# An attention layer feeding a mixture of experts: other pieces at both ends, half a superblock transposed, and a new order

## The chip, the cores and the metric

The kernel runs on one core of a Trainium2 chip. The metric is the time on the device in microseconds (us), lower is better. Engines are named as the profile names them: PE (TensorE: matmuls and transposes), DVE (VectorE), ACT (ScalarE), POOL (GpSimd) and SP (SyncE, which here only issues transfers). Each runs its own instructions strictly in the order in which they stand. All large transfers are issued by SP on one queue and are spread over the 16 DMA engines of the core.

## The reference

The output of an attention block with 32 learned queries is the input of a mixture of experts that sends each token to one expert.

```python
def mab(q, kv):                        # B 4, N 11456, m 32, C 128
    s = scale * (q @ kv.transpose(0, 2, 1))
    a = np.exp(s - s.max(-1, keepdims=True))
    a /= a.sum(-1, keepdims=True) + 1e-09
    return a @ kv
h = mab(I, x)                          # 32 queries over all tokens of a batch
x = mab(x, h).reshape(B * N, C)        # every token over the 32 rows of h
...
logits = (x / |x|) @ en.T / tau        # 8 experts
gate = softmax(logits) at its argmax
out[mask] = gate_w[mask, None] * (np.maximum(x[mask] @ w1[e], 0.0) @ w2[e])
```

## The kernel before, in words

Each of the 4 batches is cut into 6 superblocks of 1920 tokens (the last of a batch has 1856), so there are 24, numbered g = 0 to 23; batch b owns g = 6b to 6b+5. A superblock is 15 blocks of 128 tokens.

**Stage 1** (`stage1(g)`) needs every token of a batch. `load g` brings the superblock with channels on the partitions. The same tokens with tokens on the partitions come in one of two ways: for the g in `LOADED`, `loadx g` brings them from a second layout in memory; for the others PE transposes block by block (`xt g.h`) and ACT or DVE copies the result out of PSUM (`xe g.h`). `s1 g` are the scores against the 32 queries, `e1 g` the exponentials (ACT), `e1t g` a transpose (DVE), and `h g` adds to the batch's sum in PSUM.

**Between the stages** (`finish(b)`) a batch's h is normalised, small tables are made of it (`hd`, `tab`), the batch's expert is picked (`pick b`, DVE), and `loadw b` brings that expert's two weight matrices, 512 KB each. SP reads the expert's number from memory before it can issue them. `G b` and `K b` on PE multiply the weights with the small tables.

**Stage 2** (`stage2(g0, size)`) runs over groups of one or two superblocks: `s2 g` scores (PE), `am`, `e2` exponentials (ACT), `ud` two products (PE), `w`, `n2`, `dt`, and a chain of small steps up to the gate `gf`; then `F` (DVE), `eg` (POOL or DVE), `out g` (PE), two evictions `oe g.h` from PSUM (ACT or DVE) and `store g` (SP).

What sets the order is written out by hand. `ORDER` is a list of all steps; each engine runs its own steps in that order, and SP its loads and stores. `AT` gives each buffer its slot (18 slots of 960 KB hold superblocks, in and out). `BY_DVE` names the steps that DVE runs in place of their usual engine. `FILL` puts matmuls of zeros, whose result nobody reads, in front of some steps. `SPLIT` names the superblocks whose last steps and stores go in two pieces (blocks 0 to 7, 8 to 14). A load also waits until the load six before it has landed (`DEPTH`). A chain of checks at the end (`ck2` to `verdict`) sets a counter that each engine reads before the program ends.

Of the kernel before, what the change touches and what calls it, by code (L numbers as in the profile page):

```python
# [45 lines left out]
load 7, e1t 5, en7, rz 0.0, rz 0, hde 0, xe 5.0, h 5, hsb 0, s1 6, hd 0, m1 6, s1 7, sha 1, load 9, shb 1, hdc 0,
tab 0, s2 0, tabc 0, am 0, sta 0, stb 0, load 8, loadx 7, loadx 6, s2 4, vote 0, s2 1, e1 7, pick 0, e1 6, pz 1,
e2 0, e2 4, s2 2, tabs 0.0, e1t 7, loadw 0, load 10, tw 0, s2 3, s2 5, e2 2, tabs 0.1, tabs 0, am 4, am 5, e2 3,
e2 1, load 11, load 12, ud 0, am 3, uc 0, pad 17, oh 0, am 2, am 1, e1t 6, ld 0, pad 11, w 0, loadx 8, e2 5, ud 1,
ud 2, ud 3, ud 4, ud 5, uc 2, n2 0, w 1, dt 0, n2 1, zk 0, uc 3, s1 8, load 13, load 14, ln 0, ex 0, e1 8, w 2,  # L50
# [5 lines left out]
sha 2, fac 4, out 0, oe 0.0, e1t 11, zc 1, e1t 10, den 4, shb 2, oe 0.1, S 2, zr 1, rz 1.0, rz 1, h 10, h 11, lg 4,
el 4, hsb 1, v 2, gf 2, out 1, e1 12, hd 1, hdc 1, s1 14, e1t 12, F 3, S 4, pz 2, oe 1.0, s2 6, v 4, F 2, tab 1,
gf 4, tabc 1, s1 13, am 6, vote 1, pick 1, tabs 1.0, eg 3, s2 8, am 8, eg 2, sta 1, tabs 1.1, stb 1, ld 1, py 2,
e1 14, s2 9, s2 7, oe 1.1, tabs 1, am 9, e1 13, F 4, am 7, e2 6, e2 8, out 3, tw 1, oe 3.0, F 5, ad 1, e2 9, eg 4,
oe 3.1, ud 8, store 1, w 8, ud 9, e2 7, oh 1, loadw 1, dt 8, xt 12.1, xe 12.1, w 9, xt 17.0, xt 12.0, xe 17.0,  # L60
n2 8, out 4, xe 12.0, oe 4.0, eg 5, n2 9, s2 11, s2 10, load 18, md 1, oe 4.1, mdc 1, e2 11, e2 10, am 10, out 2,
ln 8, zk 1, ex 8, oe 2.0, ud 6, ud 7, uc 7, oe 2.1, ck1 0, am 11, e1t 13, dt 6, s1 16, G 1, w 6, GT 1, h 12, h 13,
e1 16, gs 1, n2 6, loadx 14, loadx 16, w 7, z 8, fac 8, load 21, gk 1, den 8, ud 10, ud 11, e1t 16, n2 7, ln 6,
ex 6, load 19, store 2, z 6, lg 8, out 5, fac 6, store 4, w 10, w 11, marg 1.0, den 6, h2 1, e1t 14, oe 5.0, lg 6,
oe 5.1, el 6, s1 18, K 1, Kc 1, s1 15, h 14, s1 17, n2 11, dt 10, K4 1, el 8, e1 15, S 6, xt 17.1, n2 10, m1 18,
marg 1.1, v 6, marg 1, e1t 15, S 8, mq 1, gf 6, xe 17.1, F 6, mx 1, xt 18.0, F 7, e1 17, K4c 1, h 15, zc 2,
load 20, h 16, xe 18.0, e1t 17, zr 2, sha 3, rz 2.0, z 10, eg 6, v 8, loadx 22, gf 8, shb 3, rz 2, out 6, h 17,
e1 18, s1 19, F 8, e1t 18, hsb 2, hd 2, hdc 2, ck1 1, oe 6.0, pz 3, oe 6.1, eg 7, xt 18.1, e1 19, ln 10, ex 10,
fac 10, den 10, out 7, xe 18.1, tab 2, tabc 2, F 9, oe 7.0, oe 7.1, store 0, eg 8, lg 10, el 10, s2 12, am 12,
vote 2, pick 2, s2 14, s2 13, s1 20, eg 9, sta 2, tabs 2.0, tabs 2.1, s2 15, stb 2, S 10, load 23, loadx 19, e2 12,  # L70
am 14, tabs 2, tw 2, e2 13, e1 20, e2 14, e1t 19, v 10, e2 15, oh 2, out 8, oe 8.1, am 13, loadw 2, gf 10, F 11,
F 10, am 15, store 5, ud 14, ud 15, uc 14, oe 8.0, eg 10, dt 14, ud 12, ud 13, w 12, n2 12, out 9, w 13, load 22,
s2 17, oe 9.0, h 18, s1 21, e2 17, dt 12, s2 16, G 2, uc 15, oe 9.1, am 17, n2 13, h 19, ld 2, eg 11, loadx 20,
w 14, e1t 20, ad 2, am 16, md 2, GT 2, n2 14, gs 2, mdc 2, e1 21, e2 16, ln 12, out 10, ex 12, oe 10.1, w 15, z 12,
store 7, store 9, store 3, ud 16, ud 17, marg 2.0, n2 15, fac 12, pad 23, gk 2, marg 2.1, e1t 21, marg 2, den 12,
zk 2, mq 2, store 6, lg 12, w 17, dt 16, w 16, K 2, s1 22, store 8, ln 14, oe 10.0, store 10, Kc 2, K4 2, e1 22,
el 12, h2 2, z 14, S 12, xt 21.0, K4c 2, xe 21.0, ex 14, n2 16, n2 17, xt 21.1, xe 21.1, xt 23.1, xt 23.0, py 3,
s1 23, v 12, fac 14, den 14, lg 14, xe 23.1, gf 12, F 13, F 12, ln 16, ex 16, hde 3, z 16, el 14, fac 16, den 16,
lg 16, xe 23.0, e1 23, el 16, eg 12, h 20, h 21, S 14, out 11, oe 11.1, e1t 22, v 14, e1t 23, mx 2, zc 3, h 22,
zr 3, h 23, S 16, v 16, rz 3.0, hsb 3, rz 3, gf 14, gf 16, F 14, out 12, oe 12.0, eg 13, hd 3, oe 11.0, hdc 3,  # L80
tab 3, tabc 3, s2 18, F 15, vote 3, pick 3, tabs 3.0, tabs 3.1, oe 12.1, store 11, eg 15, tw 3, out 13, am 18,
sta 3, tabs 3, oe 13.1, oe 13.0, eg 14, F 16, s2 19, s2 21, stb 3, loadw 3, e2 21, am 19, am 21, F 17.1, e2 18,
e2 19, s2 20, out 14, am 20, eg 16, ud 18, ud 19, w 18, F 17.0, oe 14.1, e2 20, oe 14.0, out 15, w 19, store 13,
oe 15.1, ud 20, ud 21, uc 20, dt 18, n2 19, n2 18, ln 18, dt 20, w 21, store 14, oe 15.0, eg 17.0, out 16, ex 18,
oe 16.1, s2 22, G 3, oe 16.0, out 17.0, s2 23, eg 17.1, z 18, w 20, n2 20, fac 18, den 18, lg 18, el 18, n2 21,
ln 20, GT 3, gs 3, S 18, gk 3, am 22, store 12, v 18, oe 17.0.1, ex 20, oe 17.0.0, am 23, gf 18, K 3, Kc 3,
out 17.1, z 20, e2 22, fac 20, den 20, F 18.0, K4 3, lg 20, F 18.1, oe 17.1.1, el 20, eg 18.1, oe 17.1.0, K4c 3,
F 19, ud 22, e2 23, S 20, v 20, gf 20, out 18.1, oe 18.1.1, oe 18.1.0, w 22, dt 22, ud 23, uc 23, eg 18.0,
store 15, out 18.0, F 21, dt 23, eg 19, oe 18.0.0, store 16, store 17.1, z 22, oe 18.0.1, store 17.0, ld 3, n2 22,
ad 3, F 20.1, F 20.0, eg 21, w 23, ln 22, out 19, oe 19.1, oe 19.0, ex 22, fac 22, store 18.1, eg 20.0, ck1 2,  # L90
# [805 lines left out]
```

## Time and profile before

| what | value |
|---|---|
| time, median of 3 runs | 165.62 us (163.82 to 166.64) |
| time of the profiled execution | 165.58 us |
| its span, first to last instruction | 163.4 us |
| PE busy | 152.0 us (93%) |
| DVE, ACT, POOL busy | 128.0, 111.4, 68.2 us |
| bytes moved | 62.33 MB, mean 382 GB/s |
| matmuls, of them transposes of blocks | 2086, 195 |

The profiled execution took 2.2 us more than its span, and it lies 0.04 us from the median of the three runs, so sums made against it hold for the median too. Busy shares are averages over the whole span; the rows below are cut by stage, because the load on each engine changes along the way. A busy PE is not a PE at its peak: the ends of its matmuls are modelled.

### The profile page before, as it was taken

The numbers are of one execution on the slowest core, as the hardware profiler recorded it, in microseconds if no ns is written. First come the engines' busy times: TensorE is split into PE (matmuls) and PEld (weight loads), VectorE is DVE, ScalarE is ACT, GpSimd is POOL, SyncE is SP. The second block draws the span as 40 slices with busy tenths as digits, with TensorE's granted clock in tenths as the row PEclk, the third lists the DMA queues.
The fourth block names the chain that finished last, engine by engine and source line by source line (L and its number), as shares of the span: only waits on it lengthen the run. The fifth ranks groups of instructions, "written<-read, shape, count | busy, mean of one in ns | idle before, by whom it ended". The sixth has DMA issues, their size and how long they took to land.

```text
span 163.4 us, 5394 instructions
## 1 busy us (share of the span) xinstructions
PE 152.0 (93%) x2086; PEld 82.2 (50%) x2090; DVE 128.0 (78%) x326; ACT 111.4 (68%) x244; POOL 68.2 (42%) x181
## 2 busy tenths in 40 slices
PE   7999999999999999999999999999999998898900
PEld 5658695334976634536585433738643232233400
DVE  0437664789997999989986899999878989897820
ACT  3063661966884697783878993789896899997520
POOL 8700000236664265216242634843636074884200
PEclk9999999999999999999999999999999999999995
DMA  5999999999999999999999999999997999999970
GB/s 154 394 412 423 421 423 417 418 367 419 420 423 423 412 423 382 416 421 372 305 424 331 364 413 424 422 427 431 412 394 261 330 425 419 412 373 416 408 307 19
DMA packets 10732, 62.33 MB, mean 382 GB/s; under 512 B 1352, under 2 KB 1360, under 8 KB 10704
## 3 DMA queue, kind: packets, MB, share of 16 engines
q1 hardware_dynamic: 10512, 61.94, 94.8%
q8 instruction: 17, 0.28, 0.7%
q14 instruction: 11, 0.09, 0.1%
q10 hardware_dynamic: 192, 0.02, 0.1%
HBM read 38.49 MB, written 23.46 MB: 379 GB/s over the span
## 4 chain that ended last, share of the span: by engine, by line
PE 80%; ACT 10%; DVE 3%; issue 2%; POOL 1%; DVEq 0%; POOLq 0%
PE psum L293 62%; PE psum L396 14%; ACT big L290 6%; PE psum L717 4%; ACT E L562 1%; ACT s L592 1%; ACT gf L609 1%; DVE F L620 1%; POOL E2g L622 0%; DVE am L557 0%; ACT s L593 0%; DVE Wp L582 0%; ACT ex L602 0%; DVE DT L587 0%; DVE E2g L622 0%
## 5 line engine op out<-in xcount | busy, mean ns | idle before, releaser
L290 ACT COPY big<-psum 128x960 f32<-128x960 f32 (+4 forms) x67 | 55.7, 853 | 20.9 <-PE psum L396 12.0
L622 POOL TENSOR_TENSOR E2g<-E,F 128x480 f32<-128x480 f32 (+2 forms) x24 | 25.9, 1084 | 21.8 <-PE psum L293 12.8
L293 PE MATMUL psum<-E2g,K 32*128 32x480 f32 (+2 forms) x232 | 27.5, 543 | 1.2 <-ACT big L290 0.3
L293 PE MATMUL psum<-big,ind 128*32 128x480 f32 x192 | 24.5, 571 | 0.1
L293 PE MATMUL psum<-big,E1T 128*32 128x128 f32 x720 | 24.5, 273 | 0.0
L396 PE MATMUL psum<-ident,big 128*128 128x128 f32 x195 | 24.1, 280 | 0.0
L396 PEld LDWEIGHTS psum<-ident,big 128*128 128x128 f32 x195 | 21.8, 144 | 4.1 <-issue 3.0
L293 PEld LDWEIGHTS psum<-big,E1T 128*32 128x32 f32 x720 | 21.5, 110 | 4.7 <-issue 2.3
L290 DVE COPY big<-psum 128x960 f32<-128x960 f32 (+4 forms) x17 | 18.3, 1078 | 6.8 <-PE psum L396 6.1
L293 PE MATMUL psum<-big,hd 128*32 128x480 f32 x192 | 22.0, 569 | 0.1
L293 PE MATMUL psum<-E,tG 64*64 64x480 f32 x96 | 21.6, 572 | 0.1
L293 PE MATMUL psum<-E,tD 64*64 64x480 f32 x96 | 21.6, 573 | 0.0
L426 DVE STREAM_TRANSPOSE E1T<-E 128x480 f32<-128x480 f32 x24 | 15.9, 662 | 6.3 <-ACT E L417 4.0
L417 ACT ACTIVATE E<-psum,nb 128x480 f32<-128x480 f32 x24 | 15.9, 663 | 6.2 <-PE psum L293 4.9
L562 ACT ACTIVATE E<-psum,nb 128x480 f32<-128x480 f32 x24 | 15.1, 664 | 4.2 <-PE psum L293 3.0
L557 DVE TENSOR_REDUCE am<-psum 128x1 f32<-128x480 f32 x24 | 15.2, 646 | 2.6 <-PE psum L293 1.8
L620 DVE STREAM_TRANSPOSE F<-gf 128x480 f32<-128x480 f32 (+2 forms) x29 | 16.3, 574 | 1.0 <-issue 0.5
L583 DVE TRANSPOSE_TENSOR_REDUCE n<-Wp 128x15 f32<-128x480 f32 x24 | 15.4, 653 | 0.3 <-POOL Wp L580 0.2
L293 PEld LDWEIGHTS psum<-E2g,K 32*128 32x128 f32 x232 | 9.2, 183 | 12.6 <-issue 2.3
L580 POOL TENSOR_TENSOR Wp<-U,E 128x480 f32<-128x480 f32 x9 | 10.9, 1214 | 7.6 <-ACT U L290 6.4
L293 PEld LDWEIGHTS psum<-E,tG 64*64 64x64 f32 x96 | 6.2, 132 | 12.8 <-issue 5.8
L293 PEld LDWEIGHTS psum<-big,hd 128*32 128x32 f32 x192 | 5.5, 110 | 10.1 <-issue 3.7
(135 smaller groups left out, 187.1 us busy)
## 6 DMA issues: line engine op xcount, KB each, us to landing
big<-in_xT SPq DMA_DIRECT2D x19, 960.0 KB, 13.9
out<-big SPq DMA_DIRECT2D x17, 960.0 KB, 10.8
big<-in_xP SPq DMA_DIRECT2D x11, 960.0 KB, 13.2
w<-in_w SPq DMA_DIRECT2D x8, 512.0 KB, 7.0
big<-in_xT SPq DMA_DIRECT2D x4, 928.0 KB, 7.5
out<-big SPq DMA_DIRECT2D x5, 512.0 KB, 6.6
out<-big SPq DMA_DIRECT2D x2, 928.0 KB, 10.7
out<-big SPq DMA_DIRECT2D x3, 448.0 KB, 6.4
```

Of the source, the lines that this page charges most:

```text
L290: return nc.scalar.copy(out, in_) if e == "ACT" else ENG[e].tensor_copy(out, in_)
L293: return nc.tensor.matmul(out, lhsT=lhsT, rhs=rhs, start=start, stop=stop)
L396: return [nc.tensor.transpose(flat(tp)[:, 128 * (q - q0):128 * (q - q0) + 128], v(q), ident) for q in range(q0, q1)]
L417: return [nc.scalar.activation(ap(e1), ap(ps)[:, :W], AF.Exp, bias=bt.t("nb")[:, 0:1], scale=SCALE, accum_out=bt.t("zk")[:, k:k + 1])]
L426: add(f"e1t {g}", {"DVE": 0.59}, lambda e: [nc.vector.transpose(ap(e1t), ap(e1))], [e1], [e1t])
L557: add(f"am {g}", {"DVE": 0.57}, lambda e, ps=ps, k=k: [v.tensor_reduce(t("am")[:, k:k + 1], ap(ps)[:, :W], AX.X, ALU.max, apply_absolute_v ...
L562: add(f"e2 {g}", {"ACT": 0.56}, lambda e, ps=ps, e2=e2: [nc.scalar.activation(ap(e2), ap(ps)[:, :W], AF.Exp, bias=t("nb")[:, 1:2])], [ps, ...
L580: add(f"w {g}", {"POOL": 1.21}, lambda e, ub=ub, e2=e2, wp=wp: [gp.tensor_tensor(ap(wp), ap(ub), ap(e2), ALU.mult)], [ub, e2], [wp])
L583: add(f"n2 {g}", {"DVE": 0.63}, lambda e, wp=wp, k=k: [v.tensor_reduce(t("n2")[:, k], ap(wp).rearrange("p (q i) -> p q i", i=32), AX.X, AL ...
L620: add(f"F {nm}", {"DVE": 0.09 + 0.51 * part}, lambda e, a=a, f=f, q0=q0, q1=q1: [v.transpose(ap(f).rearrange("p (q i) -> p q i", i=32)[:, ...
L622: add(f"eg {nm}", {"POOL": 0.06 + 1.15 * part, "DVE": 0.2 + 0.54 * part}, lambda e, a=a, f=f, e2=e2, e2g=e2g, c0=c0, c1=c1: [ENG[e].tensor ...
L717: fill = [nc.tensor.matmul(psum[:, s, 0:z.shape[1]], lhsT=z[:, 0:P], rhs=z, start=True, stop=True) for _ in range(n)]
```

## The change

The first loads come in smaller pieces: superblock 0 in three (4, 4 and 7 blocks, the last blocks first) where it came in two (7 and 8), superblock 1 in two where it came in one. Superblock 15 leaves `LOADED`; its first 8 blocks still come by `loadx 15`, now 512 KB, and the other 7 are transposed on PE (`HALF`). Superblocks 19 and 21 join `SPLIT`. The small inputs come in 3 transfers on ACT's queue where there were 7. The zero matmuls ahead of the first transpose go from 17 to 12. `ORDER`, `AT`, `FILL` and `BY_DVE` are new throughout.

```diff
-LOADED = [3, 6, 7, 8, 13, 14, 15, 16, 19, 20, 22]
+LOADED = [3, 6, 7, 8, 13, 14, 16, 19, 20, 22]
...
-FILL = """xt 0.0:6:17:n, tab 3:5:2:w, out 18.1:1:1:w, out 19:4:1:w, out 21:6:1:w, out 20.0:4:3:w, out 20.1:3:3:w,
-out 22.0:4:8:w, out 22.1:6:3:w, out 23.0:4:3:w, ck2:6:2:w"""
+FILL = """xt 0.0:3:12:n, tab 3:7:2:w, out 17.1:3:2:w, out 19.1:2:2:w, out 19.0:4:1:w, out 21.0:7:4:w, out 22.1:2:5:w,
+out 22.0:4:2:w, ck4:3:1:w, out 23.0:3:1:w, out 23.1:4:2:w"""
...
-SPLIT = (17, 18, 20, 22, 23)
+SPLIT = (17, 18, 19, 20, 21, 22, 23)
...
-HALF = {}
+HALF = {15: 0}
...
-FIRST = ((8, 15), (0, 8))
+FIRST = {0: ((11, 15), (7, 11), (0, 7)), 1: ((0, 8), (8, 15))}
...
-    add("ind", {"ACT": (0.6, 16e3)}, lambda e: [nc.scalar.dma_start(ind[r:r + 64], indT[r:r + 64]) for r in (0, 64)], [], [cnb])
+    add("ind", {"ACT": (0.6, 16e3)}, lambda e: [nc.scalar.dma_start(ind, indT)], [], [cnb])
...
-        return [nc.scalar.dma_start(emb_sb[r0:r1], emb[r0:r1]) for r0, r1 in ((0, 4), (4, 6), (6, 8))] + [nc.scalar.dma_start(itau[r:r + 4], tau.broadcast_to([4, 1])) for r in (0, 4)]
+        return [nc.scalar.dma_start(emb_sb, emb), nc.scalar.dma_start(itau, tau.broadcast_to([E, 1]))]
...
-        if g == 0:
-            parts = FIRST
+        if g in FIRST:
+            parts = FIRST[g]
```

Three places show what the new order moves. The first is the start of PE's instructions, from the last zero matmul on. `big` are superblocks (65 is superblock 0; 66 before and 67 after is superblock 1; 67 before and 70 after is superblock 2). `ident` marks transposes of blocks, `ind` the scores `s1`, `am` the step `sha 0`, `E1T` the step `h`. Before:

```order
L717 MATMUL psum<-zero 128x256
L396 MATMUL psum<-ident,big_65 128x128 x7
L293 MATMUL psum<-big_65,ind 32x480 x4
L396 MATMUL psum<-ident,big_65 128x128 x8
L293 MATMUL psum<-ident,am_121 32x128 x4
L396 MATMUL psum<-ident,big_66 128x128 x15
L293 MATMUL psum<-big_66,ind 32x480 x4
L293 MATMUL psum<-big_67,ind 32x480 x4
L396 MATMUL psum<-ident,big_67 128x128 x15
```

And now:

```order
L718 MATMUL psum<-zero 128x256
L397 MATMUL psum<-ident,big_65 128x128 x8
L294 MATMUL psum<-big_65,ind 32x480 x4
L397 MATMUL psum<-ident,big_65 128x128 x7
L397 MATMUL psum<-ident,big_67 128x128 x7
L294 MATMUL psum<-big_67,ind 32x480 x4
L294 MATMUL psum<-ident,am_121 32x128 x4
L397 MATMUL psum<-ident,big_67 128x128 x8
L397 MATMUL psum<-ident,big_70 128x128 x8
L294 MATMUL psum<-big_70,ind 32x480 x4
```

The eight blocks of the first two pieces are transposed before the scores, the first seven blocks of superblock 1 come ahead of `sha 0`, and `sha 0` (on which the first exponential waits) stands behind the scores of superblock 1.

The second place is SP's queue around `loadw 3`, the last weights (`w` is 512 KB each; a row of 128x1920 or 128x1856 is a whole store). Before, with stores 10 and 11 first and stores 13 and 14 last:

```order
L635 DMA out<-big_75 128x1920
L635 DMA out<-big_70 128x1856
L471 TENSOR_LOAD ei
L471 ISA x2
L473 ISA
L473 DMA w_150<-in_w 128x1024
L474 ISA
L474 DMA w_151<-in_w 128x1024
L635 DMA out<-big_80 128x1920
L635 DMA out<-big_76 128x1920
```

And now, with stores 6, 7, 11 and 12 first and stores 13 and 14 last:

```order
L636 DMA out<-big_78 128x1920
L636 DMA out<-big_77 128x1920
L636 DMA out<-big_69 128x1856
L636 DMA out<-big_70 128x1920
L472 TENSOR_LOAD ei
L472 ISA x2
L474 ISA
L474 DMA w_150<-in_w 128x1024
L475 ISA
L475 DMA w_151<-in_w 128x1024
L636 DMA out<-big_67 128x1920
L636 DMA out<-big_71 128x1920
```

Store 12 moved from behind the weights to ahead of them. Ahead of `loadw 3` stand 13 stores now, 12 before; behind it stand 11 superblocks' stores, 12 before.

The third place is the end of SP's queue. Before, from store 19 on:

```order
L635 DMA out<-big_67 128x1920
L635 DMA out<-big_72 128x1920
L635 DMA out<-big_65 128x896
L635 DMA out<-big_65 128x1024
L635 DMA out<-big_79 128x1024
L635 DMA out<-big_79 128x896
L635 DMA out<-big_81 128x1024
L635 DMA out<-big_81 128x832
L759 TENSOR_LOAD ni
```

And now, from store 19.1 on:

```order
L636 DMA out<-big_68 128x896
L636 DMA out<-big_68 128x1024
L636 DMA out<-big_72 128x1024
L636 DMA out<-big_72 128x896
L636 DMA out<-big_78 128x1024
L636 DMA out<-big_78 128x896
L636 DMA out<-big_76 128x896
L636 DMA out<-big_76 128x1024
L636 DMA out<-big_77 128x1024
L760 TENSOR_LOAD ni
L760 ISA x2
L636 DMA out<-big_77 128x832
```

Superblocks 19 (67 before, 68 now) and 21 (72 in both) go out in halves, and SP now reads the counter of the checks before it issues the last store.

## Rows read from the trace of the kernel before

**Rows 1.** The page: busy time by engine, then transfers by queue.
```profile
PE 152.0 (93%) x2086; PEld 82.2 (50%) x2090; DVE 128.0 (78%) x326; ACT 111.4 (68%) x244; POOL 68.2 (42%) x181
...
q1 hardware_dynamic: 10512, 61.94, 94.8%
q8 instruction: 17, 0.28, 0.7%
```
**Rows 2.** Windows by stage: busy us (count) per engine, clock, DMA share, GB/s.
```profile
2.00:32.00 30.00, 29.87 (x422) 20.29 (x424) 16.11 (x41) 13.07 (x32) 6.67 (x54) 1.00 1.01 406
32.00:60.00 28.00, 28.00 (x457) 16.84 (x453) 25.28 (x62) 20.01 (x47) 14.37 (x26) 1.00 1.01 412
60.00:92.00 32.00, 32.00 (x473) 17.34 (x465) 28.84 (x68) 24.06 (x53) 11.95 (x24) 1.00 0.99 375
92.00:120.00 28.00, 28.00 (x430) 15.64 (x426) 25.13 (x64) 22.54 (x51) 16.06 (x31) 1.00 1.02 422
120.00:132.00 12.00, 11.70 (x121) 3.43 (x114) 11.03 (x28) 9.75 (x16) 4.08 (x6) 1.00 0.89 327
132.00:156.00 24.00, 21.45 (x204) 7.97 (x203) 20.58 (x61) 20.32 (x50) 13.70 (x29) 1.00 1.00 409
```
**Rows 3.** The same view, finer, around the last transfers.
```profile
157.00:158.00 1.00, 0.00 (x0) 0.00 (x0) 0.00 (x0) 0.00 (x0) 0.00 (x0) 1.00 0.81 325
158.50:159.00 0.50, 0.00 (x0) 0.00 (x0) 0.00 (x0) 0.00 (x0) 0.00 (x0) 1.00 0.21 72
160.00:160.50 0.50, 0.00 (x0) 0.00 (x0) 0.00 (x0) 0.00 (x0) 0.00 (x0) 0.50 0.06 23
161.00:161.50 0.50, 0.00 (x0) 0.00 (x0) 0.00 (x0) 0.00 (x0) 0.00 (x0) 0.50 0.09 36
161.50:162.00 0.50, 0.00 (x0) 0.00 (x0) 0.00 (x0) 0.00 (x0) 0.00 (x0) 0.50 0.00 0
```
**Rows 4.** Timeline of the end: start us, us, instruction, count, idle before.
```profile
148.49 1.90 PE L717 MATMUL psum<-zwide 128*128 128x512 bf16 x8 [0.15 <-ACT big L290]
154.71 0.66 PE L293 MATMUL psum<-E2g,K 32*128 32x224 f32 x8
155.44 0.97 ACT L290 COPY big<-psum 128x448 f32<-128x448 f32 x2 [0.78 <-PE psum L658]
155.70 0.16 DVE L666 TENSOR_SCALAR fw<-fl 1x4 f32<-1x4 f32 x1
155.87 0.54 ACT L290 COPY big<-psum 128x448 f32<-128x448 f32 x1
156.43 0.33 SPq L635 DMA_DIRECT2D out<-big  x1
156.73 0.14 DVE L675 CAST ni<-fw 1x1 int32<-1x1 f32 x1
```
**Rows 5.** Timeline of PE's start.
```profile
1.05 3.81 PE L717 MATMUL psum<-zero 128*128 128x256 bf16 x17 [1.05 <-DVE zero L251]
4.65 1.61 PE L396 MATMUL psum<-ident,big 128*128 128x128 f32 x7
6.20 1.01 PE L293 MATMUL psum<-big,ind 128*32 128x480 f32 x8
7.14 1.09 PE L396 MATMUL psum<-ident,big 128*128 128x128 f32 x8
8.16 0.43 PE L293 MATMUL psum<-ident,am 128*32 128x128 f32 x8
8.52 1.86 PE L396 MATMUL psum<-ident,big 128*128 128x128 f32 x15
10.31 2.15 PE L293 MATMUL psum<-big,ind 128*32 128x480 f32 x16
```
**Rows 6.** Costliest groups: count, busy us, mean ns, idle before and its releaser.
```profile
L396 PE MATMUL psum<-ident,big 128*128 128x128 f32 x195 | 24.1, 280 | 0.0
```
**Rows 7.** Timeline of SP, with one eviction and the step `G 3`.
```profile
109.67 0.33 SPq L635 DMA_DIRECT2D out<-big  x1
...
121.18 0.33 SPq L635 DMA_DIRECT2D out<-big  x1
121.39 0.96 ACT L290 COPY big<-psum 128x960 f32<-128x960 f32 x1
124.38 0.35 SPq L473 DMA_DIRECT2D w<-in_w  x1
...
130.22 0.46 SPq L635 DMA_DIRECT2D out<-big  x1
...
133.86 0.61 PE L293 MATMUL psum<-w,hd 128*32 128x256 f32 x8
```
**Rows 8.** The weights' tile: from issue to landing, all eight transfers.
```profile
DMA to landing us min/median/max: 6.0/7.0/8.6
```
**Rows 9.** A window in which only half stores were under way: columns as in rows 2.
```profile
152.00:156.00 4.00, 3.27 (x31) 1.37 (x31) 3.03 (x12) 2.08 (x5) 0.22 (x1) 1.00 1.03 411
```

More of the change, by code (lines that the diff above doesn't have):

```diff
@@ L46 @@
[L46 to L50, printed above, removed]
@@ L56 @@
[L56 to L60, printed above, removed]
@@ L61 @@
[L61 to L90, printed above, removed]
@@ L103 @@
-00011402016274020621142e006042g6024"""
-FILL = """xt 0.0:6:17:n, tab 3:5:2:w, out 18.1:1:1:w, out 19:4:1:w, out 21:6:1:w, out 20.0:4:3:w, out 20.1:3:3:w,
-out 22.0:4:8:w, out 22.1:6:3:w, out 23.0:4:3:w, ck2:6:2:w"""
+LOADED = [3, 6, 7, 8, 13, 14, 16, 19, 20, 22]
+ORDER = """load 0.0, xt 0.0, ind, small, load 0.1, xt 0.1, load 0.2, s1 0, xe 0.1, m1 0, xe 0.0, xt 0.2, load 1.1, xt 1.1,
+xe 1.1, pad 5, xe 0.2, load 1.0, s1 1, sha 0, xt 1.0, en1, shb 0, e1 0, e1t 0, load 2, xt 2.0, load 4, s1 2, e1 1,
@@ new lines @@
+load 12, xe 10.0, e1 10, el 4, s1 11, K 0, load 15, load 17, F 1, mq 0, n2 3, ck1 0, mx 0, Kc 0, h2 0, h 8, s1 12,
+e1t 10, xe 11.1, ln 2, py 1, K4 0, h 9, eg 0, z 2, S 4, m1 12, eg 1, K4c 0, ex 2, e1 11, xe 10.1, fac 2, sha 2,
+out 0, load 14, load 13, zc 1, v 4, zr 1, e1t 11, shb 2, e1 12, gf 4, den 2, h 10, h 11, rz 1.0, rz 1, e1t 12,
+hsb 1, oe 0.0, pad 17, lg 2, load 16, oe 0.1, el 2, S 2, v 2, out 1, F 4, oe 1.0, hd 1, hdc 1, load 18, s1 14,
+s2 6, gf 2, F 3, am 6, sta 1, stb 1, s2 8, tab 1, zk 1, eg 3, tabc 1, tw 1, s2 9, vote 1, am 8, pick 1, tabs 1.0,
@@ new lines @@
+mdc 1, store 4, store 3, h 12, s1 16, m1 18, gs 1, h 13, oe 5.0, sha 3, e1 16, e1t 14, marg 1.0, marg 1.1, shb 3,
+el 6, marg 1, gk 1, pz 3, el 8, S 8, am 11, S 6, ud 10, ud 11, e1 18, mq 1, v 6, v 8, h 14, dt 10, gf 6, w 11,
+e1t 16, loadx 15, hde 3, load 20, loadx 16, load 19, F 6, mx 1, s1 15, xt 15.1, e1 15, F 7, e1t 15, w 10, xt 18.0,
+eg 6, z 10, eg 7, xe 15.1, gf 8, K 1, Kc 1, s1 17, h 15, xe 18.0, K4 1, xt 17.1, n2 10, n2 11, e1 17, K4c 1, out 6,
+e1t 17, F 8, h 16, zc 2, zr 2, oe 6.0, rz 2.0, rz 2, F 9, ln 10, ex 10, xe 17.1, h 17, hsb 2, xt 18.1, hd 2, s1 19,
@@ new lines @@
+oe 6.1, xe 18.1, eg 8, hdc 2, e1 19, s2 12, tab 2, out 7, fac 10, den 10, lg 10, el 10, e1t 18, store 2, tabc 2,
+am 12, vote 2, sta 2, pick 2, s2 15, am 15, stb 2, load 22, load 23, eg 9, S 10, oe 7.1, oe 7.0, s1 20, e1 20,
+e2 15, e2 12, s2 14, s2 13, tabs 2.0, oh 2, tabs 2.1, tabs 2, am 13, e2 13, e2 14, tw 2, pad 23, v 10, gf 10, ld 2,
+out 8, load 21, ud 12, e1t 19, ad 2, ud 13, oe 8.0, w 12, loadx 19, am 14, w 13, py 3, oe 8.1, F 11, eg 11,
+loadw 2, ud 14, ud 15, uc 15, uc 14, out 9, n2 13, F 10, dt 14, loadx 20, s2 16, oe 9.1, e2 16, n2 12, h 18, s2 17,
@@ new lines @@
+oe 21.1.0, store 21.1, out 20.1, gf 22, F 22.1, oe 20.0.0, el 23, S 23, F 22.0, eg 22.1, v 23, eg 22.0, oe 20.1.1,
+store 20.0, oe 20.1.0, gf 23, out 22.1, out 22.0, h2 1, ck1 3, marg 3.0, marg 3.1, marg 3, h2 2, mq 3, F 23.0,
+mx 3, oe 22.1.0, store 20.1, oe 22.1.1, store 22.1, ck2, ck3, ck4, ck5, F 23.1, eg 23.0, out 23.0, oe 22.0.0,
+oe 22.0.1, oe 23.0.0, eg 23.1, oe 23.0.1, verdict.0, verdict.1, verdict.2, verdict.3, verdict.4, verdict.5,
+verdict, out 23.1, store 22.0, store 23.0, oe 23.1.0, oe 23.1.1, store 23.1"""
```

64 lines of the change are left out of this document (42 added, 22 removed), and 8 rows, old and new, of the table BY_DVE.

## The prediction

> **What bounds the kernel now.** I read the page first, then windows by stage, then the timelines of both ends and of SP around the last weights.
>
> The page says that two things are nearly full at once: PE is busy 93% of the span, and the one data queue keeps the 16 DMA engines at work 94.8% of it [rows 1]. The stages say which counts where. From 2 to 120 us PE is busy 117.87 of 118 us [rows 2], with real work, since the zero matmuls lie before 4.9 us and after 121: PE sets the pace there. The transfers run beside it at up to 422 GB/s, which I take as the full rate (the stage 92 to 120) [rows 2]; the stage 60 to 92 reaches only 375, so 32 x 47 = 1504 KB, 3.6 us of transfers, were lost, and PE did not notice (32.00 of 32.00).
>
> From 120 on PE is no longer full (21.45 of 24 us in 132 to 156, part of it zero matmuls). ACT and DVE are, nearly: 20.32 and 20.58 of 24 [rows 2]. The transfers are at 409, close to full. So in the last 36 us evictions and stores set the end together: a store goes out as soon as its evictions are done, and by then the queue has little left.
>
> At the very end the last eviction, on ACT, ends at 155.44 + 0.97 = 156.41, and SP issues the last store at 156.43 [rows 4]. It is not the last thing. Until 158.5 most engines of the DMA work; from then to 161.5 only 23 to 72 GB/s move, at a share of 0.06 to 0.21, and after 161.5 nothing [rows 3]. One of 16 engines is a share of 0.0625 and 422 / 16 = 26 GB/s: about one DMA engine is 3 us behind the others, and the program waits for it. What may hold one engine back stands on the page: 17 packets of instructions took 0.7% of 16 engines' span, 0.007 x 16 x 163.4 / 17 = 1.08 us each [rows 1], on whichever engine carries them.
>
> **The change part by part.**
>
> *Seven transposes of superblock 15 on PE, 448 KB less to load.* 195 transposes took 24.1 us [rows 6], 0.124 each, so 7 cost 0.87 us in the stretch where PE is full: all of it on the path to stage 2 of the last batch. Their eviction falls to ACT, which has 28 - 22.54 = 5.5 us free in the stage 92 to 120 [rows 2]: nothing. The queue carries 458,752 bytes less: 1.09 us at 422 GB/s, on every DMA engine alike, the late one too.
>
> *The start.* PE makes zeros until 4.86, then has 7 blocks, then waits for the rest before the scores at 6.20 [rows 5]. With 12 zeros at 3.81 / 17 = 0.224 us each it is free at 1.05 + 2.69 = 3.74, and a first piece of 256 KB in place of 448 lands sooner, by at most 0.46 us at full rate. So 8 blocks, not 7, can be done before the scores, which still need the whole superblock, and 7 blocks of superblock 1 fit in before its landing. In rows 5 the work up to `sha 0`, superblock 1's transposes and its scores ends at about 11.4. In the new order I lay the same pieces end to end from the scores at 5.7 to 6.7 (the whole superblock cannot land much sooner than now): 7 blocks 0.9, 7 more 0.9, scores 1.0, `sha 0` 0.43, 8 blocks 1.0, which gives 10.9. That is 0.5 us ahead. Bounds: 0.9 ahead (five zeros fewer, all of 4.65 - 3.74), or 1.0 behind if PE's clock rises later. The zeros tell about the clock: 256 columns take 224 ns here, 512 columns take 1.90 / 8 = 238 ns near the end [rows 4, 5], so the early ones ran at the lower of the two levels, though the granted clock is shown as full; a gap in the new start could prolong that by a microsecond of work. I take 0.5, between the two, nearer to the row by row sum. PE's net is then 0.87 - 0.5 = 0.4 late, rounded, at stage 2 of the last batch.
>
> *Store 12 ahead of the last weights.* Store 10 is issued at 109.67, store 11 at 121.18, the weights at 124.38, store 12 at 130.22 [rows 7]. Its last eviction ends at 121.39 + 0.96 = 122.35, so it stood ready for 7.9 us behind the weights and stores 13 and 14, while the stage 120 to 132 ran at 327 GB/s, 12 x 95 = 1140 KB or 2.7 us short [rows 2]. Ahead of the weights it fills the hole with 960 KB, 2.33 us of transfers that are then missing at the end. The late engine may not have been idle in that hole, so its gain lies between 0 and 2.33; I take half, 1.2. What is queued behind it on SP: the weights, and behind them store 13. Who waits for the weights is `G 3` on PE (a rival below).
>
> *Stores 19 and 21 in two halves, half evictions.* A half can leave about half an eviction pair earlier, 0.5 us; four more instructions of each kind cost their fixed part on ACT and POOL. Neither is at the end itself, where 22 and 23 are cut already: 0, bounds -0.3 to +0.3. Smaller transfers: with only halves under way the queue moved 411 GB/s, against 422 for whole ones [rows 2, 9]; for 1.97 MB that is 0.1 us. The Trainium skill speaks against such cuts: its page DMA: Bandwidth & Descriptors, section Bandwidth, asks for at least 1 MiB per DMA, and gives 341 GB/s at 1 MB. By that an estimate for these two superblocks is 5.8 us in place of 4.8, 1 us lost instead of 0.1. The trace does not agree for transfers that queue behind each other (411 at half a megabyte).
>
> *The last store and the checks.* DVE now runs the checks (155.70 to 156.87, 1.2 us [rows 4]) ahead of its last eviction, and SP reads the counter ahead of the last store, so that store waits behind both. Against that the last two copies, now one after the other on ACT (0.97), run on two engines (0.54) [rows 4]. Bounds -0.4 to +1.2; the checks only need PE's transposes of small tables before the last `out`, so they overlap its wait: 0.
>
> *Small inputs in 3 transfers, not 7.* ACT has nothing to do before 9 us (13.07 busy of 30 in that stage [rows 2]): 0.
>
> *The rest of the order.* At the point where the last batch's stage 2 begins, both orders have the same 24 `h`, 13 `out`, 18 `ud` behind them. So what PE, ACT and DVE have left there is the same but for a few evictions: 0, bounds -1.5 to +1.5, from the 36 - 30.07 = 5.9 us that ACT and the 36 - 31.61 = 4.4 us that DVE are idle after 120 [rows 2], of which an order can win or lose perhaps a third.
>
> **The sum.** Evictions end at 156.41 + 0.4 = 156.8. The late engine ends 1.09 + 1.2 = 2.3 us sooner, at 159.2 in place of 161.5. Behind the last eviction the other engines took until 158.5, 2.1 us, so no end before 158.9 is possible: 159.2 stands. The profiled execution's 165.58 less 2.3 is **163.3 us**; the median of the runs is the same within 0.04.
>
> **The rivals.**
>
> *Both ends move: 161.2.* The late engine's lag goes altogether (161.5 to 158.5, 3.0 us), and the order wins 1.4 us of the free time of ACT and DVE, start and cut stores included. For it: the free time is there, and a hole filled early helps the late engine as well. Against: 1.4 us is near the end of what I allowed.
>
> *Nothing gained: 165.4.* The late engine is late because of its packets of instructions, 17 before and about as many after; it was never idle, so filling the hole does nothing for it; PE's start gains nothing either, which eats 0.87 of the 1.09. For it: it was still behind right after the slow stretch, and PE's instruction count hardly changes.
>
> *Slower, `G 3` waits for its weights: 169.* The weights took 6.0 to 8.6 us to land, so the last ones are there at 131.4 by the median, and `G 3` runs at 133.86 [rows 7, 8]. Each whole store more ahead of them, if it fills no hole, adds 2.33. One more (133.7) decides nothing; four, should stores 6, 7, 11 and 12 all still be queued, put landing at 140.7, and PE with every later step of the last batch stands 6.9 us, of which the 2.5 us that PE is idle after 132 absorb a part: 165.6 - 1.1 + 4.4 = 168.9. It decides from the second store on. Against it: the hole itself, and 13 stores ahead instead of 12.
>
> **How the numbers follow.** Forecast 0.45 (its own range 162.6 to 164.9: the whole hole filled and the start at its bound, so that evictions end at 156.4 and transfers at 158.5; or only the 1.09, with PE 0.4 late), both ends 0.25, nothing gained 0.20, slower 0.10. A measurement of this kernel tells about 2% from no change, that is 162.3 and 168.9. Faster is the first rival, 0.25; slower the last, 0.10; within 2% the other two, 0.65. The range runs from 160.9, which leaves out the far part of the first rival, to 166.5, which takes in the case of no gain with its spread and leaves out the slow one.
>
> **What would show it.** Right: PE's first transpose near 3.8; the stage 120 to 132 near 400 GB/s; last eviction near 156.8; the one-engine tail shorter than 3 us. Wrong: PE idle ahead of `G 3` with the weights as releaser; the hole at 120 to 130 as deep as before; last evictions earlier than 155.5 (first rival) or the tail as long as now.

## The result and the profile after

The changed kernel takes 167.22 us by the median of 20 runs (165.16 to 169.79), the kernel before 165.06 (163.54 to 166.93) beside it: ratio 1.0116, 95% interval 1.0076 to 1.0157, so 1.9 us slower where 2.3 us faster was forecast. On another chip it was 1.0216 (1.0154 to 1.0277). Medians are of all runs; a ratio leaves out the runs that took over 1.5% more than the fastest of their kernel. The first profile of the changed kernel is of one of its longer runs (168.51 us, mean granted clock 0.977); where a shorter one shows the same place undisturbed, the second profile (166.83 us, from the other chip) is used.

Windows by stage of the changed kernel, columns as in [rows 2]:

```profile
2.00:32.00 30.00, 27.25 (x397) 19.11 (x399) 13.53 (x31) 10.63 (x25) 6.29 (x53) 1.00 1.00 400
60.00:92.00 32.00, 32.00 (x474) 17.28 (x468) 28.12 (x66) 24.78 (x55) 14.33 (x24) 1.00 1.00 387
92.00:120.00 28.00, 28.00 (x392) 14.97 (x387) 24.10 (x61) 22.95 (x48) 11.37 (x23) 1.00 1.00 388
120.00:132.00 12.00, 12.00 (x188) 5.16 (x183) 10.26 (x34) 9.71 (x19) 5.19 (x8) 1.00 0.97 351
132.00:156.00 24.00, 22.15 (x219) 7.88 (x209) 20.60 (x57) 21.11 (x53) 18.24 (x37) 0.93 0.95 384
```

Against [rows 2], PE lost 2.6 us in the first stage (29.87 to 27.25) and is full behind it, so it cannot make that up. Its list of waits up to 121 us (engine, tile, line, releaser, us, times, longest) names the places; the last row is in the kernel before too, the others are not (the stop of 1.3 us, at the step `hd 0`, stays open below):

```profile
PE psum L294 <- DMA big<-in_xT: 1.4, 1, 1.4
PE psum L294 <- issue: 1.3, 1, 1.3
PE psum L718 <- DVE zero L252: 1.1, 1, 1.1
```

The start of PE in the second profile answers [rows 5], `G 3` answers its row in [rows 7]:

```profile
1.05 2.74 PE L718 MATMUL psum<-zero 128*128 128x256 bf16 x12 [1.05 <-DVE zero L252]
3.80 1.94 PE L397 MATMUL psum<-ident,big 128*128 128x128 f32 x8
7.33 1.83 PE L294 MATMUL psum<-big,ind 128*32 128x480 f32 x8 [1.60 <-DMA big<-in_xT]
9.09 2.37 PE L397 MATMUL psum<-ident,big 128*128 128x128 f32 x14
...
136.51 0.64 PE L294 MATMUL psum<-w,hd 128*32 128x256 f32 x8
```

The first transpose starts at 3.80, as forecast, but the scores of superblock 0 then wait 1.60 us for the third piece and run at 7.33 instead of 6.20; and these scores took 1.83 us where [rows 5] has 1.01. The end of the same profile, which answers [rows 4]:

```profile
157.88 0.66 PE L294 MATMUL psum<-E2g,K 32*128 32x224 f32 x8
158.25 0.15 DVE L669 TENSOR_TENSOR fl<-fl,fw 1x4 f32<-1x4 f32 x1
158.60 0.53 ACT L291 COPY big<-psum 128x448 f32<-128x448 f32 x1 [0.55 <-PE psum L294]
159.09 0.14 DVE L676 CAST ni<-fw 1x1 int32<-1x1 f32 x1
159.16 0.60 DVE L291 COPY big<-psum 128x448 f32<-128x448 f32 x1
...
160.54 0.33 SPq L636 DMA_DIRECT2D out<-big  x1
```

The last matmul ends at 158.54. ACT copies its half at once; DVE is still in the checks until 159.23 and copies the other half until 159.76; SP, which reads the counter ahead of the store, issues at 160.54.

These rows divide the difference of the two executions. `G 3` is 2.65 us later than in [rows 7]. From `G 3` to the end of the last matmul: 22.03 us against 21.51 ([rows 4, 7]), 0.5 more. From there to the last store's issue: 2.00 against 1.06, 0.9 more. From the issue to the end of the span: 165.1 less 160.54 against 163.4 less 156.43, 2.4 less. Outside the span lie 1.8 us instead of 2.2, 0.4 less. Sum +1.25, which is 166.83 less 165.58. Single executions differ, too: against a second profile of the kernel before (165.55 us, `G 3` at 134.62) `G 3` is only 1.9 us later, and the stretch behind the last store's issue 1.6 us shorter.

### The profile page after: what moved, and what is told of

Same layout as the page of the kernel before. It is cut to its first block, busy times and chain, and to the rows that moved or that the text cites. A ratio compares the mean times of both kernels' runs of the same rounds, so it can differ in the third digit from the quotient of the medians.

```text
span 166.7 us, 5440 instructions
## 1 busy us (share of the span) xinstructions
PE 154.3 (93%) x2103; PEld 83.1 (50%) x2103; DVE 124.2 (74%) x323; ACT 115.1 (69%) x252; POOL 70.9 (43%) x187
## 4 chain that ended last, share of the span: by engine, by line
PE 81%; DVE 5%; POOL 3%; DMA 3%; issue 2%; ACT 2%; SPq 0%; POOLq 0%
PE psum L294 64%; PE psum L397 14%; DMA big<-in_xT 3%; PE psum L718 3%; POOL E2g L623 2%; ACT big L291 1%; DVE big L291 1%; DVE n L584 1%; DVE am L558 1%; SPq L373 0%; DVE F L621 0%; DVE gf L609 0%; DVE Wp L583 0%; POOL Wp L581 0%; POOL z L596 0%
## 5 line engine op out<-in xcount | busy, mean ns | idle before, releaser
L291 ACT COPY big<-psum 128x960 f32<-128x960 f32 (+4 forms) x75 | 59.5, 821 | 14.9 <-PE psum L397 8.8
L623 POOL TENSOR_TENSOR E2g<-E,F 128x480 f32<-128x480 f32 (+2 forms) x30 | 29.0, 974 | 24.6 <-DVE F L621 14.6
L294 PE MATMUL psum<-E2g,K 32*128 32x480 f32 (+2 forms) x248 | 28.4, 529 | 1.9 <-ACT big L291 0.8
L294 PE MATMUL psum<-big,ind 128*32 128x480 f32 x192 | 25.4, 570 | 1.4 <-DMA big<-in_xT 1.4
L397 PEld LDWEIGHTS psum<-ident,big 128*128 128x128 f32 x202 | 22.5, 144 | 6.7 <-issue 3.4
L397 PE MATMUL psum<-ident,big 128*128 128x128 f32 x202 | 25.8, 281 | 0.0
L294 PE MATMUL psum<-big,hd 128*32 128x480 f32 x192 | 22.8, 570 | 0.0
L291 DVE COPY big<-psum 128x960 f32<-128x960 f32 (+4 forms) x15 | 14.8, 994 | 8.3 <-PE psum L397 5.7
L294 PEld LDWEIGHTS psum<-E2g,K 32*128 32x128 f32 x248 | 10.1, 187 | 16.1 <-POOL E2g L623 4.2
L581 POOL TENSOR_TENSOR Wp<-U,E 128x480 f32<-128x480 f32 x9 | 10.9, 1214 | 7.5 <-ACT U L291 6.2
L601 POOL TENSOR_TENSOR lg<-DT,den 128x240 f32<-128x240 f32 (+1 forms) x13 | 7.8, 605 | 9.4 <-DVE den L599 5.8
```

The costliest lines, as they stand in the source:

```text
L291: return nc.scalar.copy(out, in_) if e == "ACT" else ENG[e].tensor_copy(out, in_)
L294: return nc.tensor.matmul(out, lhsT=lhsT, rhs=rhs, start=start, stop=stop)
L397: return [nc.tensor.transpose(flat(tp)[:, 128 * (q - q0):128 * (q - q0) + 128], v(q), ident) for q in range(q0, q1)]
L581: add(f"w {g}", {"POOL": 1.21}, lambda e, ub=ub, e2=e2, wp=wp: [gp.tensor_tensor(ap(wp), ap(ub), ap(e2), ALU.mult)], [ub, e2], [wp])
L601: add("lg " + nm, {"POOL": 0.64}, lambda e: [gp.tensor_tensor(u("lg"), dv(), u("den").rearrange("p a q -> p q a").unsqueeze(3).broadcast_t ...
L623: add(f"eg {nm}", {"POOL": 0.06 + 1.15 * part, "DVE": 0.2 + 0.54 * part}, lambda e, a=a, f=f, e2=e2, e2g=e2g, c0=c0, c1=c1: [ENG[e].tensor ...
```

## The experiments

Ratios are to the kernel before on the same chip; those under one heading shared a chip. Of these headings the changed kernel itself ran only under the second, so the other runs are held against it by their ratios (its own were 1.0116 and 1.0216). 1% is 1.65 us.

### Four single edits of the changed kernel

*Checks last.* In the order:

```diff
 oe 23.0.1,
-verdict.0, verdict.1, verdict.2, verdict.3, verdict.4, verdict.5, verdict,
 out 23.1, store 22.0, store 23.0, oe 23.1.0, oe 23.1.1, store 23.1
+verdict.0, verdict.1, verdict.2, verdict.3, verdict.4, verdict.5, verdict
```

> The changed kernel with the seven small steps of the last check (verdict) written behind the last store, not ahead of the last eviction; nothing else differs. My theory: in the changed kernel they stand in DVE's way (159.82 to 160.98, so that the last DVE eviction ends at 161.51 though its matmul was done at 160.28) and the counter is read by SP ahead of the last store (0.77 us after the eviction). So the last store goes out about 1.3 us after the last matmul's eviction could have allowed it: 1.0 to 1.3 us less, 166.0 by the median, ratio to the kernel before near 1.005. Rival: the last transfer is not what the end waits for, then no change, 167.2.

165.00 us, ratio 1.0021 (0.9979 to 1.0062): by the ratio 1.6 us less than the changed kernel's first runs, on another chip, and more than forecast. Its end:

```profile
156.21 0.66 PE L293 MATMUL psum<-E2g,K 32*128 32x224 f32 x8
156.94 0.53 ACT L290 COPY big<-psum 128x448 f32<-128x448 f32 x1 [0.55 <-PE psum L293]
156.94 0.62 DVE L290 COPY big<-psum 128x448 f32<-128x448 f32 x1 [0.45 <-PE psum L293]
157.48 0.15 DVE L666 TENSOR_SCALAR fw<-fl 1x4 f32<-1x4 f32 x1
...
157.63 0.33 SPq L635 DMA_DIRECT2D out<-big  x1
```

Both copies start together, and the store goes out 0.76 us after the matmul, not 2.00. In all six profiles with the checks ahead this distance is 1.98 to 2.00, in all seven with the checks behind 0.75 or 0.76: 1.25 us. Behind the store, whose transfer hides them, the checks cost little: from the store's issue to the end 4.8 to 5.2 us (6.0 in one profile) against 4.5 to 4.8 with the checks ahead, so some 0.4 us come back there at the median.

*Zeros in the tail.*

```diff
-out 22.1:2:5:w
+out 20.0:2:2:w, out 20.1:6:3:w, out 22.1:2:5:w
```

> The changed kernel with five more zero matmuls, two ahead of out 20.0 and three ahead of out 20.1, where PE was idle for 0.50 and 0.84 us just before the granted clock fell to half at 152.2. Theory: the fall of the clock between 152 and 156 goes, the mean granted clock is 0.985 or more in nearly every run (in the changed kernel 9 of 20 runs are below 0.98, and these are 1.5 us longer), and the median is 0.5 to 0.8 us lower, 166.5. Rival one: PE's clock in the tail is hidden by ACT and DVE, which are the bound there, so the clock stays up and the time does not move. Rival two: the zeros stand in the way of out 20.1, +0.3 us.

166.89 us, ratio 1.0126 (1.0058 to 1.0194): no gain that can be measured in six runs. One of them is below a mean clock of 0.98.

*Two pieces.* Superblock 0 as 7 and 8 blocks, its steps merged in the order (`xt 0.1` and `xt 0.2` become one, `load 0.2` goes).

```diff
-FIRST = {0: ((11, 15), (7, 11), (0, 7)), 1: ((0, 8), (8, 15))}
+FIRST = {0: ((8, 15), (0, 8)), 1: ((0, 8), (8, 15))}
```

> The changed kernel with superblock 0 in two pieces as before (7 and 8 blocks) and superblock 1 still in two. Theory: the scores of superblock 0 wait 1.42 us at 5.64 because the third piece lands late on two of the DMA engines (6.9 instead of about 5.7); with two pieces they run near 6.2 and not at 7.05, and that 0.8 us stays to the end: 166.4. Rival: the late landing comes from something else that shares the engines in the first 7 us (small inputs, packets of instructions), then the second piece lands at 6.5 or later as well and the time stays at 167.2 or rises by the blocks that can no longer be turned early (up to 0.5).

165.75 us, ratio 1.0053 (1.0010 to 1.0096). The scores ran at 6.25. The transfers were slow just while the third piece was due: in all seven profiles with three pieces they moved 190 to 248 GB/s between 5 and 6 us, in all six with two pieces in this order 398 to 420. (One of the seven, with 223, still had its piece in time.) The same microsecond (PE busy, clock, DMA share, GB/s) in the second profile of the changed kernel and in *three undone* (below), which has two pieces:

```profile
5.00:6.00 1.00, 0.74 (x4) 1.00 0.64 190
```

```profile
5.00:6.00 1.00, 1.00 (x10) 1.00 1.03 418
```

Why they are slower with three pieces is not shown.

*15 whole.* `xt 15.1` and `xe 15.1` go from the order.

```diff
-LOADED = [3, 6, 7, 8, 13, 14, 16, 19, 20, 22]
+LOADED = [3, 6, 7, 8, 13, 14, 15, 16, 19, 20, 22]
-HALF = {15: 0}
+HALF = {}
```

> The changed kernel with superblock 15 loaded whole again: PE has 7 transposes and ACT one eviction less, the queue 448 KB more. Theory, by which PE is what is late from 5 us to the end: 0.87 us less on PE, so the last batch starts 0.9 us sooner and the time falls by 0.5 to 0.9, 166.5. Rival, by which the transfers set the end: 448 KB at 400 GB/s are 1.1 us more, 168.3.

166.18 us, ratio 1.0052 (1.0009 to 1.0094). 448 KB more to load, and not slower; that it is faster by about 1 us the overlapping intervals do not show.

### The changed kernel again, and three edits together

The changed kernel without an edit:

> The changed kernel as it is, run beside the variants so that they have it on the same chip. Theory: 166.6 to 167.3, ratio near 1.012. In the profile the scores of superblock 0 wait for the third piece (6.8 to 7.7, as in the three profiles with three pieces); the last store is issued about 1.3 us after the last matmul plus one eviction. Whether PE's stop at hd 0 for 1.3 us and the fall of the granted clock in the tail come back is open: both came in some profiles and not in others, and if neither comes here, they are no part of the median.

167.42 us, ratio 1.0216 (1.0154 to 1.0277). The third piece was late again; PE's stop at `hd 0` did not come back; four of six runs had a mean clock under 0.98.

*Three undone:* the diffs of checks last, two pieces and 15 whole in one kernel.

> Three things of the change undone together: checks behind the last store, superblock 0 in two pieces, superblock 15 loaded whole; the order, the cut stores and store 12 ahead of the weights stay. Theory, by which these three are separate losses of 1.6, 1.0 and 1.0 us (what each gave alone) and the rest of the change is worth 1.7 us: 163.4, ratio 0.990 (0.985 to 0.995). Rival: they hide behind each other (whichever ends last), so that the three together give little more than the largest alone: 165.0, ratio 1.000.

164.10 us, ratio 0.9970 (0.9932 to 1.0008). 2.4% less than the changed kernel on this chip, though not the 0.990 of the separate sums: what is left of the change is not told from nothing. In its profile `G 3` is at 133.5, 3 us sooner than in the changed kernel's, and 1.5 us of that are lost again in the tail, where the granted clock fell to half in this execution.

*Store 12 behind*, on top of the three undone:

```diff
-out 15, w 19, store 12, ud 20,
+out 15, w 19, ud 20,
...
-store 14, store 15,
+store 14, store 12, store 15,
```

> As the kernel with the three undone, but store 12 goes behind store 14 again, so behind the last weights. Theory of the prediction (store 12 fills a hole at 120 to 132 and is missing at the end): 1.2 us slower than that kernel, up to 2.3, ratio near 1.000. Rival, since the stores of the tail now wait for their evictions and not for the queue: no difference, within 0.3, and the weights land a little sooner.

164.25 us, ratio 0.9972 (0.9929 to 1.0015): no difference at all. Windows of the two, three undone first:

```profile
120.00:132.00 12.00, 11.71 (x125) 3.74 (x122) 10.74 (x32) 9.55 (x18) 5.61 (x9) 1.00 0.94 340
```

```profile
120.00:132.00 12.00, 11.70 (x175) 4.92 (x174) 10.43 (x34) 10.08 (x17) 6.38 (x9) 1.00 0.81 295
```

With store 12 behind, the hole is deeper by 12 x 45 = 540 KB, and nobody waits for it.

*Uncut*, on top of the three undone: 19 and 21 leave `SPLIT`; of their two gates, products and matmuls the later place is kept (for the matmul of 21 the earlier), the three zero matmuls ahead of the two matmuls of 19 stand together ahead of its one, and one copy each goes to DVE.

```diff
-SPLIT = (17, 18, 19, 20, 21, 22, 23)
+SPLIT = (17, 18, 20, 22, 23)
```

> As the kernel with the three undone, but superblocks 19 and 21 go whole through gate, matmul, eviction and store again (not in halves). If the cuts are where the change gains, 0.5 to 1.5 us slower than with them, since a whole store leaves later and more bytes stand in the queue at the end; by the prediction's term for them 0, within 0.3; if small transfers cost (the Trainium skill's page DMA: Bandwidth & Descriptors, section Bandwidth), an estimate by that page is 1 us faster.

168.11 us, ratio 1.0223 (1.0174 to 1.0272), 2.5% slower than with the cuts. The timeline shows where:

```profile
148.02 1.88 POOL L620 TENSOR_TENSOR E2g<-E,F 128x480 f32<-128x480 f32 x2 [1.92 <-DVE F L618]
149.27 1.09 PE L291 MATMUL psum<-E2g,K 32*128 32x480 f32 x8 [2.35 <-ACT s L590]
151.73 1.68 PE L291 MATMUL psum<-E2g,K 32*128 32x256 f32 x12 [1.37 <-ACT s L591]
```

PE stops twice, for 2.35 and 1.37 us, where the cut kernel has 0.51 and 0.84. For the first of these matmuls the load of its weights names POOL's gate product as releaser (2.84 us), and POOL had waited 1.92 us for DVE's `F`. So the chain of gates, products and copies got longer; since the whole steps stand at the later place, how much of that is the size and how much the place is not separated. Transfers of twice the size gave nothing back that could be seen. An estimate of 1.5 of the 4.1 us is the granted clock (from the stretch with and without its fall, last section), which fell behind these stops: all six runs have a mean below 0.98. With another order around them whole superblocks might do better, as in the kernel before.

### Zeros, and what pieces and half cost without the rest

*Zeros ahead of the scores*, in the changed kernel:

```diff
-xt 0.0:3:12:n
+xt 0.0:3:12:n, s1 0:3:6:n
```

> The changed kernel with six narrow zero matmuls ahead of the scores of superblock 0, which lie in PE's wait for the third piece (5.7 to 7.3). In one profile of the changed kernel the scores behind that wait took 1.83 us and the 14 transposes after them 2.37, in the other 1.01 and 1.75: 1.44 us for the clock alone. Theory: with PE at work in the wait the scores take 1.01 us in every profile, and the median falls by 0.5 to 0.9 (half the runs pay 1.44 now): ratio 0.004 below that of the changed kernel, which lies at 1.012 to 1.022 by the chip. Rival: the zeros are no better than the wait, no change; or they stand ahead of the scores when the piece lands early, +0.3.

165.58 us, ratio 1.0108 (1.0047 to 1.0168). It lies on the right side, but the intervals overlap, and in its one profile the third piece happened to be in time (scores at 5.91). The time does not settle it.

*All mended:* the three undone, three more zeros at the start, and the five zeros of the tail:

```diff
-xt 0.0:3:12:n
+xt 0.0:3:15:n
-out 22.1:2:5:w
+out 20.0:2:2:w, out 20.1:6:3:w, out 22.1:2:5:w
```

> The three undone (checks behind, two pieces, 15 whole), and zeros added: 15 in place of 12 ahead of the first transposes, and the five of the tail ahead of out 20.0 and 20.1. Theory: PE's start as in the best profile (scores of superblock 0 near 5.9, 1.01 us), no fall of the clock in the tail in most runs, so below the three undone by 0.5 to 1.0: 163.3, ratio 0.991. Rival: the last transfers become the limit (in the kernel before 6.9 us from the last store's issue to the end, against 4.8 here), so what the evictions gain comes back there, ratio 0.997.

163.05 us, ratio 0.9929 (0.9900 to 0.9958): faster than the kernel before, and by the ratio than the changed one. Its stages to 32 us and from 132:

```profile
2.00:32.00 30.00, 29.86 (x424) 19.78 (x426) 15.43 (x40) 12.62 (x30) 7.18 (x57) 1.00 1.01 410
...
132.00:156.00 24.00, 22.65 (x227) 8.31 (x219) 19.24 (x56) 21.29 (x55) 17.17 (x37) 1.00 0.94 382
```

PE loses nothing at the start, the clock is full to the end of the tail, and all 12 runs have a mean clock of 0.989 or more.

*Three pieces in it*, with the steps and the order of the change there:

```diff
-FIRST = {0: ((8, 15), (0, 8)), 1: ((0, 8), (8, 15))}
+FIRST = {0: ((11, 15), (7, 11), (0, 7)), 1: ((0, 8), (8, 15))}
-xt 0.0:3:15:n
+xt 0.0:3:12:n, s1 0:3:6:n
```

> As the one with all mended, but superblock 0 in three pieces, with six zeros in PE's wait for the third. Theory: the third piece still lands at 6.8 to 7.7, so the scores are 1 us later than with two pieces: ratio +0.006. Rival: what the three pieces cost was only the late clock, which the zeros cure: no difference.

164.09 us, ratio 0.9977 (0.9940 to 1.0014): 0.8 us more than all mended. The scores took 1.01 us, but ran at 7.29, behind 0.57 us of wait that the zeros did not fill; below them those of all mended:

```profile
7.29 1.01 PE L293 MATMUL psum<-big,ind 128*32 128x480 f32 x8 [0.57 <-DMA big<-in_xT]
```

```profile
6.24 1.01 PE L293 MATMUL psum<-big,ind 128*32 128x480 f32 x8
```

*Half of 15 in it*, `xt 15.1` and `xe 15.1` back in the order:

```diff
-LOADED = [3, 6, 7, 8, 13, 14, 15, 16, 19, 20, 22]
+LOADED = [3, 6, 7, 8, 13, 14, 16, 19, 20, 22]
-HALF = {}
+HALF = {15: 0}
```

> As the one with all mended, but superblock 15 half loaded, half turned on PE, as in the change. Theory by which PE is the limit until 120 and the evictions after it: 0.87 us slower, ratio +0.005. Rival by which the transfers set the end of this quicker kernel: 448 KB less, 1.1 us faster, ratio -0.006.

163.66 us, ratio 0.9974 (0.9944 to 1.0004): 0.7 us more. `G 3` at 133.93 instead of 133.53, although the scores of superblock 0 ran 0.39 us sooner in this execution (5.85).

### Two terms of the prediction, in the kernel before

The kernel before without an edit:

> The kernel before as it is, for a second profile. By the prediction's view the late engine belongs to the kernel: from the last store's issue to the end 6.5 to 7.0 us again, with 20 to 70 GB/s over the last 2 to 3 us. Rival: it was the chance of one execution; then 4.5 to 5.5 us.

164.62 us, ratio to itself 0.9977 (0.9929 to 1.0025). The late engine is there again. Its last windows, as in [rows 3]:

```profile
158.00:159.00 1.00, 0.00 (x0) 0.00 (x0) 0.00 (x0) 0.00 (x0) 0.00 (x0) 1.00 1.01 402
159.00:160.00 1.00, 0.00 (x0) 0.00 (x0) 0.00 (x0) 0.00 (x0) 0.00 (x0) 0.59 0.30 97
160.00:161.00 1.00, 0.00 (x0) 0.00 (x0) 0.00 (x0) 0.00 (x0) 0.00 (x0) 0.50 0.10 40
161.00:162.00 1.00, 0.00 (x0) 0.00 (x0) 0.00 (x0) 0.00 (x0) 0.00 (x0) 0.50 0.04 18
```

Two microseconds at 18 to 40 GB/s, 6.2 us from the last store's issue (157.17) to the end.

*Store 12 ahead*, in the kernel before:

```diff
-oe 12.1, store 11, eg 15,
+oe 12.1, store 11, store 12, eg 15,
...
-gk 3, am 22, store 12, v 18,
+gk 3, am 22, v 18,
```

> The kernel before with store 12 behind store 11, so ahead of the last weights, and nothing else. The prediction's term: 1.2 us faster (0 to 2.33), ratio 0.993, with 120 to 132 us near 400 GB/s instead of 327. Rival, after what it did in the new order: no difference, ratio 1.000 within 0.003.

164.43 us, ratio 0.9976 (0.9931 to 1.0022): 0.4 us, not told from nothing.

*Half of 15*, in the kernel before: the same lines of `LOADED` and `HALF` as in the change, and

```diff
-e1 15, S 6,
+e1 15, xt 15.1, xe 15.1, S 6,
```

> The kernel before with superblock 15 half loaded, half turned on PE (7 transposes after e1 15, one eviction on ACT). The prediction's terms: 448 KB are 1.09 us less for the DMA engines, and PE's 0.87 us lie beside; 1.1 us faster, ratio 0.993. Rival, as in the new order: PE's 0.87 us reach the end, ratio 1.004.

166.34 us, ratio 1.0112 (1.0045 to 1.0179). Its last store is issued at 158.53, 2.1 us later than in [rows 4], and the span ends at 162.8: 4.3 us behind the issue and no longer 6.9. This execution is the shortest of its six (165.06 us); by the ratio the edit costs 1.8 us.

*Both:*

> The kernel before with both edits. The prediction's sum of the two is 2.3 us faster: ratio 0.986. Rival: 1.004, what PE pays for superblock 15 alone.

165.17 us, ratio 1.0005 (0.9959 to 1.0050). Issue at 159.13, end 4.0 us behind it. The forecast sum of 2.3 us is not there in the kernel for which it was made. But store 12 is not nothing beside the half: with it ahead the median fell from 166.34 to 165.17, 1.2 us, as the prediction had it (the intervals of the two ratios just overlap). Why it counts there and not alone is not shown.

## Why the prediction was wrong

Its reading of the bound holds from 32 to 120 us, where PE is idle for at most 0.8 us in every profile here; before 32 it is not full in the changed kernel, and what is lost there shows at `G 3` (27.25 us busy and `G 3` at 136.77 in the first profile, 29.86 and 133.53 with all mended). Its late engine came back in the second profile of the kernel before. What failed is the sum, which took the transfers for the end and let PE and the evictions be 0.4 us late beside them. They came 3.0 us later (last eviction at 159.76, forecast 156.8), and SP issued the store 0.78 us behind it, against 0.02 in [rows 4]. The queue had run nearly empty by then (49 GB/s from 160.50 to 161.00), and the end followed the last store by the 4.5 to 5.2 us (6.0 in one profile) that it takes in the new order. That this stretch is 2.4 us shorter than in [rows 4], where the term for the late engine gave 2.3, is luck: against the second profile of the kernel before it is 1.6, and in the new order neither half of the term moves it by more than 0.3 us (4.8 with 15 whole, 4.5 in the changed kernel; 4.9 with store 12 behind, 4.8 with it ahead). The half of superblock 15 in the kernel before shows the exchange in one execution: the store 2.1 us later, the end following it 2.6 us sooner, and by the ratio nothing won.

*The start, forecast -0.5, bound +1.0.* The step that failed first. The row by row sum comes to 10.9 only with the scores starting at 5.7, half a microsecond ahead of [rows 5], and that is all of its 0.5; it goes against its own remark that "the whole superblock cannot land much sooner than now". That remark was right and still too kind: the superblock landed later. In six of seven profiles with three pieces the scores waited for the third, to 6.84 at the earliest and 7.67 at the latest (6.20 in [rows 5], 5.83 to 6.44 with two pieces in six profiles of the new order). Three pieces against two, the rest of the three undone: 0.8 us. The second part, "PE's clock rises later", was named, priced at up to 1.0 and not chosen: in three of thirteen profiles of the new order the scores took 1.83 us and not 1.01, and the transposes behind them up to 2.60, not 1.86. In the second profile that is 0.82 + 0.62 = 1.44 us. It does not belong to the third piece: two of the three have two pieces, and waits of 1.42 to 2.10 us ahead of the scores went without it in four others. In none of the four profiles with more zeros at the start did it happen, against three of the nine without; that is too few to show that the zeros are the reason.

*Seven transposes, +0.87, "against" 1.09 of transfers.* The size was right (0.7 us, *half of 15 in it* against *all mended*). That transfers would pay for it was wrong: taken alone in the kernel before it cost 1.1% (0.45 to 1.79%), and with store 12 ahead too the two together gained nothing.

*Store 12 ahead of the weights, -1.2.* Its largest term, and not there: no difference in the new order, 0.4 us (-0.4 to 1.1) in the old; only beside the half of superblock 15 in the old order did the move bring the 1.2, and that stays open. The stage 120 to 132, expected near 400 GB/s, moved 351. The hole is real, but in the new order the tail waits for evictions that are not done yet. Bytes moved earlier are not missed at the end if the queue then idles.

*Last store behind the checks, 0.* The step with the clearest answer, 1.25 us at the store's issue, just over the bound of 1.2 that the text itself gave. The reason offered for zero, that the checks overlap PE's wait, looked at when they are ready (158.3 us in the first profile, well ahead) and not at their place in DVE's order: behind its copy `oe 23.0.0` and ahead of `oe 23.1.0`, so they ran when the last copy was due. The wait of SP for the counter came on top.

*Cut stores, 0.* What they do was missed: without them, with the whole steps at the later place, the new order was 4.1 us slower, an estimated 1.5 of it the granted clock. By the Trainium skill's page DMA: Bandwidth & Descriptors, section Bandwidth, an estimate was 1 us lost; the run with whole stores was the slower one, so nothing here shows that loss.

*The rest of the order, 0, bounds 1.5.* From `G 3` to the last matmul 22.03 us, not 21.51: 0.5, inside the bounds. The cut stores lie in that stretch as well, so what the rest of the order costs alone is not separated. The small inputs as three transfers were not tried apart.

*The rivals.* The slow one had the right side and the wrong place: in no profile did `G 3` wait for its weights; it was late because PE was. The list of what would make the forecast wrong looked for an idle PE only ahead of `G 3`, not at its start.

Open: PE's stop of 1.31 us at `hd 0` in the first profile, 0.86 and 0.57 in two others, with no releaser that the profile shows, and absent in the rest. Open too why 0.4 us less lies outside the span in all profiles of the new order.
